# Four remainder loads on GpSimd's queue, tile 1 of x on the sync queue, and a new order of the first transposes

## The chip, the cores and the metric

The kernel runs on one core of a Trainium2 chip. The metric is the device time of one execution in microseconds. A core has a matrix engine (TensorE, PE in the profile, with its weight loads shown apart as PEld), VectorE (DVE), ScalarE (ACT), GpSimd (POOL) and SyncE (SP). Loads and stores are issued by SP, ACT or POOL into queues and are carried out by 16 DMA engines.

## The reference

An input x of 2048 tokens by 448 features is normalized; a linear attention with 16 heads of 28 and a two-layer network are applied to the result, and their product is added to x:

```python
def _A_ref(x, wqkv, wo):
    B, S, D = x.shape
    H = 16; Dh = D // H
    qkv = (lambda x, *d: x.transpose(*d))((x @ wqkv).reshape(B, S, 3, H, Dh), 2, 0, 3, 1, 4)
    q, k, v = qkv[0], qkv[1], qkv[2]
    phi = lambda t: jnp.where(t > 0, t + 1, jnp.exp(t)) + 1e-6
    pq, pk = phi(q), phi(k)
    kv = jnp.einsum("bhsd,bhse->bhde", pk, v)
    z = jnp.einsum("bhsd->bhd", pk)
    num = jnp.einsum("bhqd,bhde->bhqe", pq, kv)
    den = jnp.einsum("bhqd,bhd->bhq", pq, z)[..., None] + 1e-6
    o = num / den
    return (lambda x, *d: x.transpose(*d))(o, 0, 2, 1, 3).reshape(B, S, D) @ wo

def _B_ref(x, w1, b1, w2, b2):
    h = jnp.einsum("bsd,df->bsf", x, w1) + b1
    r = jnp.where(h > 0, h, 0)
    return jnp.einsum("bsf,fd->bsd", r * r, w2) + b2

xn = _layernorm(x)
return x + _A_ref(xn, ...) * silu(_B_ref(xn, ...))
```

The hidden width F is 1792. All inputs and the output are bf16.

## The kernel before

The 2048 tokens are 16 tiles of 128 (`NT`), four of which make a group (`NG`). Each of the first stages needs xT, the normalized x with the features on the partitions. The 448 features are three full chunks of 128 and a last one of 64. A product over 448 features therefore has three full steps and one of 64 rows. The last chunk is kept twice in xT, in rows 0 to 63 and in rows 64 to 127, and so are the last 64 rows of the weights. Two products with 64 rows each can then run side by side in the two halves of the matrix. The two copies of the last 64 weight rows are loaded apart from the main load: the code calls these two loads `twins` (L414 in `load_k`, L434 in `load_w1`).

The program is a list of operations with what they read and write. `schedule` (L88) simulates them and fixes the order of each engine's instructions: PE and SP keep the order in which the operations were added, while DVE, ACT and POOL take the operation with the earliest due time among those that are ready in the simulation. `after` and `prio` of an operation tie it to a place in that order, and they are no waits on the chip. In `schedule` a load occupies a single simulated DMA pipe (L218 to L222). `emit` (L231) turns the dependences into semaphore waits.

The change lies in the head of the program, in which the tiles 0 to 3 are handled one by one:

- Loads. `load_x(0, 1)` on SP, `load_x(1, 2, "act")` on ACT, then on SP the main k weights (`wk`, 384 KB), tiles 2 and 3, the two main loads of the first four h blocks (`w1a`, 192 KB each), the two k twins (64 KB each), the two h twins (32 KB each), tiles 4 to 7, and the remaining weights (L441 to L450).
- Statistics. `ln_stats` (L461) and `ln_rstd` (L467) give mean and 1/std of a tile: `st` and `mv` on DVE, `ln` and `ex` on ACT.
- Normalization. `ln_norm` (L482) writes features 0 to 383 of tiles 0 to 3, in two parts (256 and 128 columns) for tiles 0 and 1. `ln_last` (L506) writes the last 64 features twice, in one DVE operation of 128 columns. For tiles from 4 on, `ln_norm` writes 448 columns and `ln_twin` (L497) copies the last 64.
- Transposes. `pe_transpose` (L519) transposes the chunks of a tile on PE into a PSUM bank and copies them to xT on the engine named; `turn(si, part, eng)` (L1072) does it for half a tile. Its four operations of a tile use the names `xT00`, `xT01` and so on in the table `head`.
- First products. k of tiles 0 and 1 (`k0`, `k1`), and the first four h blocks, whose left half of 256 tokens (tiles 0 and 1) is `first` and whose right half (tiles 2 and 3) is `second`. `mains` (L596) issues full steps, `rests` (L607) the 64-row steps of two products side by side: these are the remainders, and they are the first users of the twins. After them comes `pe_four(*second)`, which needs xT of tiles 2 and 3.
- `warm` (L1056) issues matmuls on constants ahead of the first transposes.
- The two strings at L1109 and L1110 fix the order of the head's operations on DVE and ACT by name (`xd` is the doubled last chunk, `xn` the normalized part).

The masks that POOL builds (`zmask`, L383 to L387) are used in the middle of the program, at 75.9 us.

Of the kernel before, what the change touches and what calls it, by code (L numbers as in the profile page):

```python
# [10 lines left out]
S, D, F = 2048, 448, 1792  # L11
# [6 lines left out]
RATE = 300e3  # L18
# [37 lines left out]
class Program:  # L56
# [31 lines left out]
    def schedule(self):  # L88
# [59 lines left out]
        while n:  # L148
# [68 lines left out]
            op.start = st  # L217
            if op.nbytes:  # L218
                free[e] = st + op.dur
                s2 = max(dma_free, st + 1.75)  # L220
                dma_free = s2 + op.nbytes / RATE
                op.end = dma_free + 0.3  # L222
            else:
                op.end = st + du
                free[e] = op.end
# [62 lines left out]
def bass_recurrent_scan__linear_attn_block__dense_activation_squared_relu__prompt_kernel(  # L288
# [4 lines left out]
    with ExitStack() as es:  # L293
# [106 lines left out]
        def dma(eng, dst, src, writes, nbytes, reads=()):  # L400
            return add(eng, lambda e, _: e.dma_start(dst, src), reads, writes, 0.5, nbytes=nbytes)

        def load_x(lo, hi, eng="sp", reads=()):
            names = [("x", i) for i in range(lo, hi)]
            return dma(eng, x_tok[:, lo:hi, :], x_r[:, lo:hi, :], names, (hi - lo) * P * D * 2, reads)

        def load_k(eng, w, src, name, lo, hi, eng2=None, reads=(), later=False):

            n = (hi - lo) * 2
            dma(  # L410
                eng, w[:, 0:3, lo:hi], src[0:384, lo:hi].rearrange("(c p) j -> p c j", p=P), [(name, 0)], 384 * n,
                reads,
            )
            def twins():  # L414
                for i in (0, 1):
                    dma(eng2 or eng, w[64 * i : 64 * i + 64, 3, lo:hi], src[384:448, lo:hi], [(name, 1 + i)], 64 * n)

            if later:
                return twins
            twins()  # L420

        def load_w1(name, lo, hi, parts=1, between=()):


            for i in range(parts):
                n = (hi - lo) // parts
                c = slice(lo + i * n, lo + (i + 1) * n)
                dma(
                    "sp", w_1[:, 0:3, c], B_w1[0:384, c].rearrange("(c p) j -> p c j", p=P), [(name, 3 * i)], 768 * n
                )  # L430
            for todo in between:
                todo()
            mid = (lo + hi) // 2
            for i, c in ((0, slice(lo, mid)), (1, slice(mid, hi))):  # L434
                dma("sp", w_1[64 * i : 64 * i + 64, 3, c], B_w1[384:448, c], [(name, 1 + i)], 64 * (hi - lo))

        w1_of = lambda fi: "w1a" if fi < 4 else "w1b" if fi < 8 else "w1c"
        wnames = lambda name: [(name, i) for i in range(4 if name == "w1a" else 3)]
        table = add("act", lambda e, _: e.preload_act_table_set("natural_log_exp_and_others"), [], ["actw"], 0.1)
        table.prio = -120  # L440
        load_x(0, 1)  # L441
        load_x(1, 2, "act").prio = -118
        twins = load_k("sp", w_qkv, A_wqkv, "wk", 384, 2 * D, later=True)
        load_x(2, 4)
        dma("act", b1r[0:NF, :], B_b1.rearrange("(f p) -> f p", p=P), ["b1r"], F * 2, ["b1r"]).prio = -115
        load_w1("w1a", 0, 512, 2, [twins])
        load_x(4, 8)
        load_w1("w1b", 512, 1024)
        load_k("sp", w_qkv, A_wqkv, "wq", 0, 384)
# [30 lines left out]
            )  # L480

        def ln_norm(si, part=None):  # L482
            c = (slice(0, D if si > 3 else 384), slice(0, 256), slice(256, 384))[0 if part is None else part + 1]
            return add(
                "dve",
                lambda e, _: e.tensor_scalar(
                    out=xn[:, si, c], in0=x_tok[:, si, c], scalar1=mv[:, si, 0:1],
                    scalar2=rstd[:, si : si + 1], op0=ALU.subtract, op1=ALU.mult,
                ),
                [("x", si), ("mv", si), ("rstd", si)], [("xn", si) if part is None else ("xn", si, part)],  # L490
                0.4 if part is None else (0.22, 0.18)[part],
            )
# [554 lines left out]
        for i in range(4):  # L1047
            head[f"st{i}"], head[f"mv{i}"] = ln_stats(i)
            head[f"ln{i}"], head[f"ex{i}"] = ln_rstd(i, i + 1)
            for j in (0, 1) if i < 2 else (None,):  # L1050
                head[f"xn{i}" + ("" if j is None else str(j))] = ln_norm(i, j)
            twin = head[f"xd{i}"] = ln_last(i)
        for op in masks:
            op.after = [twin]

        def warm(n, wide=False, after=()):  # L1056
            b = Buf("W")
            w = 512 if wide else P

            def f(e, _):  # L1060
                for _i in range(n):
                    last = e.matmul(ps(b)[:, 0:w], junk[:, 0:P], junk[:, 0:w], start=True, stop=True)
                return last

            add("pe", f, ["ones", *after], [b], n * (0.426 if wide else 0.107))

        warm(8, wide=True)
        k0, k1 = kk(0), kk(1)
        first = [hh(0, fi, 0) for fi in range(4)]
        second = [hh(0, fi, 1, first[fi].bank) for fi in range(4)]  # L1070
# [7 lines left out]

        turn(0, 0, "act")
        turn(0, 1, "act")  # L1080
        turn(1, 0, "act")
        mains(k0, (0,), [("xT", 0, "a")] + wnames("wk")[:1])
        mains(k0, (1,), [("xT", 0, 0)])
        mains(k0, (2,), [("xT", 0, 1)])
        turn(1, 1, "act")
# [8 lines left out]
        )  # L1094
        h_mains(0, (2,))
        h_mains(1)
        h_mains(2)
        head["xT2"] = pe_transpose(2, None, "act")
        h_mains(3)
        head["xT3"] = pe_transpose(3, None, "dve")  # L1100
        n = len(pr.ops)
        rests(k0, k1)
        k0.out()
# [2 lines left out]
        rests(first[0], first[2])  # L1106
        rests(first[1], first[3])
        for eng, names in (
            ("dve", "st0 mv0 st1 mv1 xn00 xn01 xd0 xn10 xn11 xd1 st2 mv2 st3 mv3 xd2 xn2 xd3 xn3 xT3"),  # L1109
            ("act", "ln0 ex0 ln1 ex1 xT00a xT00 xT01 xT10 xT11 ln2 ex2 ln3 ex3 b1 xT2"),  # L1110
        ):
            ops = [head[n] for n in names.split()]
            for i, op in enumerate(ops):
                op.after = ops[:i]
                op.prio = -100 + i
        for op in early:
            op.after = [head["xT3" if op.eng == "dve" else "xT2"]]
        pe_four(*second)

        def quads(g, what):  # L1120
# [16 lines left out]
        for g, (first, second) in enumerate(streams):  # L1137
            if g + 1 < NG:
                n = len(pr.ops)
                ln(4 * g + 4, 4 * g + 8)  # L1140
                if g == 0:
                    for op in pr.ops[n:]:
                        if op.writes[0][0] == "st":
                            op.after = [head["xT3"]]
            quads(g, first)
            for i in range(4 * g, 4 * g + 4):
                if i:
                    zsum(i)
            if g + 1 < NG:
                for si in range(4 * g + 4, 4 * g + 8):  # L1150
                    dma_transpose(si)
                    if si == 5:
                        load_x(8, 12)
            if g == 0:
                load_x(12, 16)
                late_loads()
            quads(g, second)
            rest_transpose(2 * g)
            rest_transpose(2 * g + 1)
# [86 lines left out]
```

## Time and profile before

| What | Value |
|---|---|
| Median of 3 runs | 141.42 us (141.3 to 141.51) |
| The profiled execution, its time | 141.34 us |
| Its span on the page | 139.7 us |
| TensorE clock granted | 1.00 in every stretch |
| Data moved by DMA | 12.91 MB, mean 92 GB/s |
| DMA engines' share in the first 10 us | 0.85, 256 GB/s |
| First 10 us: busy PE, DVE, ACT, POOL | 9.51, 7.15, 6.29, 2.35 us |

The page of the profile gives busy times of the engines; a line of a group names the line of the code, the engine, the operation, the tile it writes and the tiles it reads. POOL's work in the head ends at 3.25 us, after which it has none until 66.67 us. SP's queue issues without a pause from 0.0 to about 10.8 us and then waits for work until 13.59 us. In that time it issues the four twin loads from 2.44 to 4.92 us and tiles 4 to 7 at 4.96 us.

### The profile page before, as it was taken

The numbers are of one execution on the slowest core, as the hardware profiler recorded it, in microseconds if no ns is written. First come the engines' busy times: TensorE is split into PE (matmuls) and PEld (weight loads), VectorE is DVE, ScalarE is ACT, GpSimd is POOL, SyncE is SP. The second block draws the span as 40 slices with busy tenths as digits, with TensorE's granted clock in tenths as the row PEclk, the third lists the DMA queues.
The fourth block names the chain that finished last, engine by engine and source line by source line (L and its number), as shares of the span: only waits on it lengthen the run. The fifth ranks groups of instructions, "written<-read, shape, count | busy, mean of one in ns | idle before, by whom it ended". The sixth has DMA issues, their size and how long they took to land.

```text
span 139.7 us, 3106 instructions
## 1 busy us (share of the span) xinstructions
PE 136.6 (98%) x1255; PEld 68.0 (49%) x1255; DVE 92.2 (66%) x226; ACT 77.8 (56%) x152; POOL 25.0 (18%) x33
## 2 busy tenths in 40 slices
PE   9999999999999999999999999999999999999992
PEld 2474444444444444444455455645555555555481
DVE  3989899799878994889995900329636071542653
ACT  4769787879988878979788912422033030301220
POOL 6000000000000000000893000000002328091770
DMA  6997367999723200000000148960000103111122
GB/s 190 247 335 219 77 170 186 356 276 144 131 52 70 60 6 0 0 19 5 0 0 0 42 120 169 175 107 0 0 0 5 66 0 101 35 66 66 38 99 68
DMA packets 20354, 12.91 MB, mean 92 GB/s; under 512 B 9524, under 2 KB 19956, under 8 KB 20340
## 3 DMA queue, kind: packets, MB, share of 16 engines
q1 hardware_dynamic: 18332, 11.52, 33.3%
q10 hardware_dynamic: 2008, 1.20, 4.3%
q8 instruction: 10, 0.16, 0.5%
q14 instruction: 4, 0.03, 0.1%
HBM read 8.78 MB, written 2.10 MB: 78 GB/s over the span
## 4 chain that ended last, share of the span: by engine, by line
PE 95%; DVE 2%; DMA 2%; issue 0%; DVEq 0%
PE pb L955 31%; PE pb L688 30%; PE pb L641 9%; PE pb L1021 8%; PE pb L722 7%; PE pb L672 6%; DMA x_tok<-in_A_x_dram 2%; PE pb L528 1%; PE pb L728 1%; DVE st L463 1%; PE pb L815 1%; PE pb L776 1%; PE pb L853 0%; DVE xn L991 0%; DVE mv L464 0%; PE pb L846 0%
## 5 line engine op out<-in xcount | busy, mean ns | idle before, releaser
L688 PE MATMUL pb<-xT,w 64*128 64x512 bf16 (+2 forms) x408 | 51.6, 365 | 0.0
L955 PE MATMUL pb<-w,r 64*128 64x448 bf16 (+3 forms) x406 | 44.9, 343 | 0.0
L697 ACT ACTIVATE r<-pb,b1f 128x512 bf16<-128x512 f32 x56 | 35.1, 688 | 4.2 <-PE pb L688 4.2
L688 PEld LDWEIGHTS pb<-xT,w 64*128 64x128 bf16 (+1 forms) x408 | 22.8, 94 | 22.5 <-ACT r L697 0.5
L955 PEld LDWEIGHTS pb<-w,r 64*128 64x128 bf16 (+1 forms) x406 | 22.8, 95 | 19.9 <-issue 0.7
L966 DVE TENSOR_TENSOR gbuf<-pb,b2b 128x448 bf16<-128x448 f32 (+1 forms) x16 | 9.2, 608 | 30.0 <-PE pb L955 30.0
L931 ACT ACTIVATE gbuf<-gbuf 128x448 bf16<-128x448 bf16 (+1 forms) x16 | 8.7, 565 | 36.0 <-DVE gbuf L966 35.5
L1000 POOL TENSOR_TENSOR xn<-xn,x_tok 128x448 bf16<-128x448 bf16 x15 | 15.0, 1032 | 46.3 <-DVE xn L991 46.3
L641 PE MATMUL pb<-w_qkv,xT 64*128 64x512 bf16 (+1 forms) x106 | 17.8, 376 | 0.0
L672 PE MATMUL pb<-xT,w_qkv 64*128 64x512 bf16 x84 | 15.5, 376 | 0.0
L705 DVE TENSOR_TENSOR r<-r 128x512 bf16<-128x512 bf16 x42 | 14.4, 418 | 0.0
L390 POOL MEMSET kvm<- 128x2048 bf16 x1 | 1.8, 1804 | 63.4 <-DVE zb L666 63.4
L1021 PE MATMUL pb<-msb,pqT 64*128 64x448 bf16 (+3 forms) x93 | 10.9, 343 | 0.0
L629 DVE SCALAR_TENSOR_TENSOR qk<-pb,qk 128x512 bf16<-128x512 f32 x16 | 10.6, 685 | 0.2
L463 DVE BATCH_NORM_STATS2 st<-x_tok 128x6 f32<-128x448 bf16 x16 | 9.3, 610 | 2.0 <-DMA x_tok<-in_A_x_dram 2.0
L991 DVE TENSOR_TENSOR xn<-pb,gbuf 128x448 bf16<-128x448 f32 (+2 forms) x17 | 9.2, 591 | 2.0 <-ACT gbuf L931 1.5
L619 ACT ACTIVATE qk<-pb 128x512 bf16<-128x512 f32 x16 | 8.9, 593 | 3.0 <-PE pb L641 2.5
L641 PEld LDWEIGHTS pb<-w_qkv,xT 64*128 64x128 bf16 (+1 forms) x106 | 6.7, 94 | 6.0 <-ACT xT L538 0.2
L722 PE MATMUL pb<-qk,xn 128*128 128x448 bf16 x48 | 9.3, 353 | 0.0
L619 ACT ACTIVATE pqT<-pb 128x512 bf16<-128x512 f32 x12 | 6.8, 597 | 3.2 <-PE pb L688 1.6
L672 PEld LDWEIGHTS pb<-xT,w_qkv 64*128 64x128 bf16 x84 | 6.0, 94 | 5.0
L706 ACT ACTIVATE r<-r 128x512 bf16<-128x512 bf16 x14 | 8.4, 637 | 0.0
(71 smaller groups left out, 99.7 us busy)
## 6 DMA issues: line engine op xcount, KB each, us to landing
out_dram<-xn SPq DMA_DIRECT2D x15, 112.0 KB, 1.7
w<-in_B_w_dram SPq DMA_DIRECT2D x1, 1568.0 KB, 10.0
x_tok<-in_A_x_dram SPq DMA_DIRECT2D x3, 448.0 KB, 3.8
xT<-rows ACTq DMA_DIRECT2D x6, 112.0 KB
w<-in_B_w_dram SPq DMA_DIRECT2D x1, 576.0 KB, 4.6
xT<-rows SPq DMA_DIRECT2D x5, 112.0 KB
w_o<-in_A_wo_dram SPq DMA_DIRECT2D x1, 392.0 KB, 11.3
w_qkv<-in_A_wqkv_dram SPq DMA_DIRECT2D x1, 384.0 KB, 3.6
```

The source lines that it names most:

```text
L463: add("dve", lambda e, _: e.bn_stats(st6[:, si, :], x_tok[:, si, :]), [("x", si)], [("st", si)], 0.58),
L619: add("act", lambda e, _: e.activation(out=slot, in_=src(), func=AF.Exp), [buf, "actw"], [tile], 0.6)
L629: lambda e, _: e.scalar_tensor_tensor(out=slot, in0=src(), scalar=1.0 + 1e-6, in1=slot, op0=ALU.add, op1=ALU.max),
L641: return e.matmul(ps(b)[:, 0:512], xT[half[h], c, si * P : (si + 1) * P], w_qkv[half[h], c, 384 : 2 * D], start=start, stop=stop,)
L672: return e.matmul(ps(b)[:, 0:512], w_qkv[half[h], c, m * P : (m + 1) * P], xT[half[h], c, g * 512 : (g + 1) * 512], start=start, stop=stop,)
L688: return e.matmul(ps(b)[:, c0 : c0 + n], w_1[half[h], c, fi * P : (fi + 1) * P], xT[half[h], c, t : t + n], start=start, stop=stop,)
L697: lambda e, _: e.activation(out=slot, in_=ps(b)[:, 0:512], func=AF.Relu, bias=b1f[:, fi : fi + 1]),
L705: return e.tensor_tensor(out=slot, in0=slot, in1=slot, op=ALU.mult)
L722: last = e.matmul(ps(b)[:, 0:D], xn[:, si, c * P : (c + 1) * P], pk_of(si), start=(si == 0), stop=(si == NT - 1),)
L955: return e.matmul(ps(b)[:, 0:n], r2[half[h], fi, si * P : (si + 1) * P], w_2[half[h], fi, c], start=start, stop=stop)
L1000: eng, lambda e, _: e.tensor_tensor(out=ob, in0=ob, in1=x_tok[:, si, c], op=ALU.add),
L1021: return e.matmul(ps(b)[:, 0:n], q, m, start=start, stop=stop)
```

## The change

- The k twins and the twins of `w1a` are issued on POOL instead of SP. Each now reads `("wk", 0)`, so that POOL waits until the main k weights have landed.
- The planner's model gives a load on POOL a landing 3.0 us after its start, without the shared pipe.
- Tile 1 of x is loaded on SP, directly behind tile 0, instead of on ACT.
- For tiles 1 to 3, the main normalization now writes all features (tile 1: 256 and 192 columns; tiles 2 and 3: 448) and `ln_twin` copies the last 64; tile 0 is as before. The order in the string for DVE is changed to match: `xn` ahead of `xd`.
- Two small matmuls follow the eight of `warm`.
- On PE, the first transposes of tile 1 follow the first k step of tile 0 instead of preceding it; the transposes of tile 2 precede the third h block instead of following it.
- The transposes of tile 3 are made in two halves: the first is copied by DVE, the second by ACT. What had been tied to `xT3` is tied to `xT30` on DVE, and to `xT31` on ACT where it had been tied to `xT2`.

```diff
--- before.py
+++ after.py
@@ -217,9 +217,12 @@
             op.start = st
             if op.nbytes:
                 free[e] = st + op.dur
-                s2 = max(dma_free, st + 1.75)
-                dma_free = s2 + op.nbytes / RATE
-                op.end = dma_free + 0.3
+                if e == "pool":
+                    op.end = st + 3.0
+                else:
+                    s2 = max(dma_free, st + 1.75)
+                    dma_free = s2 + op.nbytes / RATE
+                    op.end = dma_free + 0.3
             else:
                 op.end = st + du
                 free[e] = op.end
@@ -413,7 +416,7 @@
             )
             def twins():
                 for i in (0, 1):
-                    dma(eng2 or eng, w[64 * i : 64 * i + 64, 3, lo:hi], src[384:448, lo:hi], [(name, 1 + i)], 64 * n)
+                    dma(eng2 or eng, w[64 * i : 64 * i + 64, 3, lo:hi], src[384:448, lo:hi], [(name, 1 + i)], 64 * n, twin_after)
 
             if later:
                 return twins
@@ -432,18 +435,24 @@
                 todo()
             mid = (lo + hi) // 2
             for i, c in ((0, slice(lo, mid)), (1, slice(mid, hi))):
-                dma("sp", w_1[64 * i : 64 * i + 64, 3, c], B_w1[384:448, c], [(name, 1 + i)], 64 * (hi - lo))
+                dma(
+                    "pool" if name == "w1a" else "sp", w_1[64 * i : 64 * i + 64, 3, c], B_w1[384:448, c], [(name, 1 + i)],
+                    64 * (hi - lo), twin_after if name == "w1a" else (),
+                )
 
         w1_of = lambda fi: "w1a" if fi < 4 else "w1b" if fi < 8 else "w1c"
         wnames = lambda name: [(name, i) for i in range(4 if name == "w1a" else 3)]
         table = add("act", lambda e, _: e.preload_act_table_set("natural_log_exp_and_others"), [], ["actw"], 0.1)
         table.prio = -120
+        twin_after = [("wk", 0)]
         load_x(0, 1)
-        load_x(1, 2, "act").prio = -118
-        twins = load_k("sp", w_qkv, A_wqkv, "wk", 384, 2 * D, later=True)
+        load_x(1, 2)
+        twins = load_k("sp", w_qkv, A_wqkv, "wk", 384, 2 * D, "pool", later=True)
+        twin_after = [("wk", 0)]
         load_x(2, 4)
         dma("act", b1r[0:NF, :], B_b1.rearrange("(f p) -> f p", p=P), ["b1r"], F * 2, ["b1r"]).prio = -115
         load_w1("w1a", 0, 512, 2, [twins])
+        twin_after = ()
         load_x(4, 8)
         load_w1("w1b", 512, 1024)
         load_k("sp", w_qkv, A_wqkv, "wq", 0, 384)
@@ -480,7 +489,7 @@
             )
 
         def ln_norm(si, part=None):
-            c = (slice(0, D if si > 3 else 384), slice(0, 256), slice(256, 384))[0 if part is None else part + 1]
+            c = (slice(0, D), slice(0, 256), slice(256, D if si else 384))[0 if part is None else part + 1]
             return add(
                 "dve",
                 lambda e, _: e.tensor_scalar(
@@ -1049,7 +1058,7 @@
             head[f"ln{i}"], head[f"ex{i}"] = ln_rstd(i, i + 1)
             for j in (0, 1) if i < 2 else (None,):
                 head[f"xn{i}" + ("" if j is None else str(j))] = ln_norm(i, j)
-            twin = head[f"xd{i}"] = ln_last(i)
+            twin = head[f"xd{i}"] = ln_twin(i, i + 1, "dve") if i else ln_last(i)
         for op in masks:
             op.after = [twin]
 
@@ -1065,6 +1074,7 @@
             add("pe", f, ["ones", *after], [b], n * (0.426 if wide else 0.107))
 
         warm(8, wide=True)
+        warm(2)
         k0, k1 = kk(0), kk(1)
         first = [hh(0, fi, 0) for fi in range(4)]
         second = [hh(0, fi, 1, first[fi].bank) for fi in range(4)]
@@ -1078,8 +1088,8 @@
 
         turn(0, 0, "act")
         turn(0, 1, "act")
+        mains(k0, (0,), [("xT", 0, "a")] + wnames("wk")[:1])
         turn(1, 0, "act")
-        mains(k0, (0,), [("xT", 0, "a")] + wnames("wk")[:1])
         mains(k0, (1,), [("xT", 0, 0)])
         mains(k0, (2,), [("xT", 0, 1)])
         turn(1, 1, "act")
@@ -1094,10 +1104,11 @@
         )
         h_mains(0, (2,))
         h_mains(1)
+        head["xT2"] = pe_transpose(2, None, "act")
         h_mains(2)
-        head["xT2"] = pe_transpose(2, None, "act")
         h_mains(3)
-        head["xT3"] = pe_transpose(3, None, "dve")
+        turn(3, 0, "dve")
+        turn(3, 1, "act")
         n = len(pr.ops)
         rests(k0, k1)
         k0.out()
@@ -1106,15 +1117,15 @@
         rests(first[0], first[2])
         rests(first[1], first[3])
         for eng, names in (
-            ("dve", "st0 mv0 st1 mv1 xn00 xn01 xd0 xn10 xn11 xd1 st2 mv2 st3 mv3 xd2 xn2 xd3 xn3 xT3"),
-            ("act", "ln0 ex0 ln1 ex1 xT00a xT00 xT01 xT10 xT11 ln2 ex2 ln3 ex3 b1 xT2"),
+            ("dve", "st0 mv0 st1 mv1 xn00 xn01 xd0 xn10 xn11 xd1 st2 mv2 st3 mv3 xn2 xd2 xn3 xd3 xT30"),
+            ("act", "ln0 ex0 ln1 ex1 xT00a xT00 xT01 xT10 xT11 ln2 ex2 ln3 ex3 b1 xT2 xT31"),
         ):
             ops = [head[n] for n in names.split()]
             for i, op in enumerate(ops):
                 op.after = ops[:i]
                 op.prio = -100 + i
         for op in early:
-            op.after = [head["xT3" if op.eng == "dve" else "xT2"]]
+            op.after = [head["xT30" if op.eng == "dve" else "xT31"]]
         pe_four(*second)
 
         def quads(g, what):
@@ -1141,7 +1152,7 @@
                 if g == 0:
                     for op in pr.ops[n:]:
                         if op.writes[0][0] == "st":
-                            op.after = [head["xT3"]]
+                            op.after = [head["xT30"]]
             quads(g, first)
             for i in range(4 * g, 4 * g + 4):
                 if i:
```

## The prediction

> **What bounds the kernel now.** I read the page first, then the chain that ended last for the first 12 us, then each engine's order of instructions in that stretch, then the loads' landings, since the diff touches only the head and loads that the head waits for. The page gives the bound:
>
> ```profile
> PE 136.6 (98%) x1255; PEld 68.0 (49%) x1255; DVE 92.2 (66%) x226; ACT 77.8 (56%) x152; POOL 25.0 (18%) x33
> ...
> PE 95%; DVE 2%; DMA 2%; issue 0%; DVEq 0%
> ```
>
> TensorE is never without work once it has started: from 9 us to 130 us its records are gapless. A gain can therefore come only from starting this stream earlier or closing holes in the head, and a hole made in the head goes to the end undiminished. The chain shows the head; columns are start, duration and piece:
>
> ```profile
> 0.00 2.20 DMA x_tok<-in_A_x_dram
> 2.20 0.02 issue
> 2.22 0.64 DVE st L463
> ...
> 3.07 0.52 DVE st L463
> 3.59 0.02 issue
> 3.61 0.18 DVE mv L464
> 3.80 0.24 DVE xn L486
> 4.04 0.05 issue
> 4.09 1.00 PE pb L528 x6
> 5.08 0.65 PE pb L641 x3
> ...
> 8.10 0.22 PE pb L528 x4
> 8.32 0.32 PE pb L641 x2
> 8.64 1.90 PE pb L688 x32
> 10.54 0.86 PE pb L641 x8
> ```
>
> Tile 0's arrival at 2.20 starts everything. The statistics of tile 1 sit between those of tile 0 and the first normalization, so the DVE sets the 4.09. The two pieces at 8.32 and 8.64 hold the first k remainders (L641 x2), and the h remainders ahead of the second h quarter: these need the twin loads that the change moves. One hole is named by the weight loads:
>
> ```profile
> 8.84 1.42 PEld L688 LDWEIGHTS pb<-xT,w 64*128 64x128 bf16 x28 [0.26 <-DVE xT L537]
> ```
>
> The second h quarter waits for tile 3's copy (DVE, 8.36 to 8.78) and begins at 8.84. Then the twins' present landing (issue columns: count, KB each, us from issue to landing; windows at their issue):
>
> ```profile
> w_qkv<-in_A_wqkv_dram SPq DMA_DIRECT2D x2, 64.0 KB, 3.9
> ...
> w<-in_B_w_dram SPq DMA_DIRECT2D x2, 32.0 KB, 3.0
> ```
>
> Narrower windows give 2.44 + 4.1 = 6.5 us and 3.05 + 3.7 = 6.75 us for k, and 6.9 and 7.0 us for h. Their users come at 8.26 and 8.48. They are more than 1.2 us early: moving them off SP frees no wait on the path.
>
> **What the skill says.** The Trainium skill, "DMA: Bandwidth & Descriptors", section "Anatomy of one DMA — SWDGE (gpsimd) path", prices a load from GpSimd, whose descriptors software writes, at about 2.0 us plus bytes over 436 GB/s. No load here is issued there, so no trace confirms it. "Issuing engines are not separate DMA queues" on that page says that all issuers use the same 16 engines and another issuer saves issue time only; the trace agrees that issue time is the small part (0.57 us per SP issue against 2.7 to 4.1 us to land). "SBUF — State Buffer", section "SBUF: two separate sides", says that GpSimd and two-port VectorE operations exclude each other, and (in "A bandwidth-pool intuition that's wrong (but worth ruling out)") that a GpSimd load of 620 ns took 3100 ns beside one. This trace shows such exclusion for GpSimd's own operations:
>
> ```profile
> L367 POOL TENSOR_SCALAR_AFFINE_SELECT hmask<-hmask x2: 295/2377/4459, 68.7 to 73.2; 128x112 f32<-128x112 f32 x2
> ```
>
> One select took 295 ns and its equal 4459 ns, while 19 squares (L705) ran back to back on the DVE, each still 419 ns. GpSimd lost, the DVE lost nothing.
>
> **Part by part.** The sum is made against the profiled execution, 141.34 us (span 139.7 and 1.6 around it), which lies 0.08 under the median of 141.42.
>
> *x 1 on SP behind x 0.* At present the two share the engines: from 1.5 to 1.8 us SP's queue moved 0.05 MB and ACT's 0.04. Adding up the traffic in steps of 0.1 us gives 117 KB by 1.7 us, tile 0's size; shared, it needed until about 1.9. So x 0 lands some 0.2 us sooner (bounds 0 and 0.3). Tile 1, issued 0.3 later, comes at about 2.6, before the DVE wants it (2.98 less 0.2). The other side: the k main load is issued at 0.9, not 0.44. The engines stay loaded from 1.6 on, so I put it at 4.1 instead of 4.04; its user started at 4.92, or 4.7 shifted. Nothing lost. x 2 and 3 may slip from 4.71 to 4.9, just where the DVE asks; the following rstd is held by ACT until later.
>
> *Normalization.* Tiles 1 to 3 lose the doubled last chunk (312 ns) for a wider main one (374 to 392 ns for 448 columns) and a 64-column copy (181 ns by L666): about 0.11 us less DVE each. Worth nearly nothing: xn of tile 2 is started by rstd (ACT, 6.68), not by DVE time.
>
> *T 1 behind the first k main, T 2 before h 2.* Nothing is added; 0.22 us of matmul pass T 1, whose copy then ends about 0.2 later and holds k 1 by 0.1 us (cost 0.1, bounds 0 and 0.15). T 2 issued before h 2 meets xn of tile 2 just as it is ready: a hole of at most 0.1, closed because T 3 then no longer has to wait. The two small warm matmuls fill PE's idle time before 4.09 and cost at most 0.05.
>
> *T 3 in halves.* The DVE copies 256 columns instead of 512 (425 ns before; half saves about 0.15), ACT the rest in 381 ns. ACT starts later by a transpose, and T 3's second half may wait 0.05 for the bank that T 2's copy frees. The later half decides: ready at about 8.63 shifted, instead of 8.78. Together with the earlier start the head gains 0.2 us: the second h quarter could begin at 8.64. Bounds of this gain: 0.05 and 0.35.
>
> *Four twin loads on GpSimd.* They wait for the k main load, so the first can be taken up at 4.15. Behind the waiting instruction on POOL stand only the other three and the zmask operations, wanted first at 75.9. SP, relieved of four issues (2.4 us), issues x 4 to 7 and all that follows 2 us sooner; their users come late, and PE behind 9 us has no hole that this could fill. All that counts is when the last h twin, t4, is in. PE then needs 0.05 plus two paired 256-column steps (0.21) before the second quarter, which began at 8.84: the change in time is t4 - 8.58, and never better than -0.2.
> - Low: spacing as SP's, 0.57, and the skill's price of 2.15 for 64 KB (2.08 for 32): t4 = 4.15 + 1.7 + 2.1 = 8.0, in time.
> - Middle: spacing 0.8, between that 0.62 and the 1 us to the first byte that the DMA page states under Specifications, and a landing of 2.7, the shortest that the same 32 KB had on SP under this load: 4.15 + 2.4 + 2.7 = 9.25, so +0.67.
> - High: the DVE's normalizations run unbroken from 4.2 to 5.0 and from 6.6 to 7.6 in the new order; if they shut GpSimd out as L705 did, 1.2 us more: t4 = 10.5, so +1.9.
> I take the middle, since 8.0 needs the best of both and the engines move some 345 GB/s in this stretch (4.0 to 5.0 us), with 1.66 MB issued on SP by 2.9 us in the new order still ahead of or beside the twins. Result: 141.34 + 0.67 = 142.0.
>
> **The rivals.**
> 1. Twins late by a moderate amount (forecast): +0.3 to +1.1, 142.0 us. For it: four serial issues from 4.15, each needing over 2 us. Chance 0.38.
> 2. GpSimd is shut out by the DVE, or holds DVE back in turn on the first tiles: +1.2 to +2.5, about 143. For it: the 4459 ns select. Against it: statistics lie between the normalizations (5.0 to 6.4) and leave gaps for three issues. Chance 0.18.
> 3. Other side: the twins are in before PE reaches the h remainders. One mechanism, a free ring of their own instead of a place behind 384 KB of h weights, so landings of 2.1 us; it decides if t4 is under 8.4. Then the gain of x 0's earlier landing remains, -0.2 (to -0.35): 141.1. Against it: the spacing. Chance 0.24.
> 4. Gain and delay cancel (t4 near 8.6), 141.4, within the bound. Chance 0.20.
>
> **How the numbers follow.** A measurement of this kernel tells about 0.2% from no change, 0.28 us. Slower: 1 and 2 and a remnant of 4, 0.57. Rival 3 has most of its mass beyond 0.2%, counting extra gain from the earlier loads that I did not find: faster 0.20. Within: 0.23. The range takes rival 3 to -0.3 (141.05) and two thirds of rival 2 (143.1). The likeliest case alone spans 141.6 to 142.5.
>
> **What would show it.** Right: PE has a hole of 0.4 us or more between T 3 and the h remainders, put down to a w load from POOL, and the second h quarter starts after 9.1; first normalization 0.2 earlier; POOL's issues 0.6 to 1.0 apart. Wrong: remainders directly behind T 3 (then the issues or landings are cheaper than assumed), an x 0 that still lands at 2.2, DVE normalizations above 400 ns (GpSimd holding the port), or a changed time outside the span.

## The result and the profile after

The changed kernel takes 147.2 us (median of 6 runs, 145.12 to 147.82), the kernel before 141.47 us (6 runs beside it). The ratio is 1.0347, with a 95% interval of 1.0274 to 1.0421. The ratio is formed from the runs within 1.5% of the fastest of their kernel, three of the six after, so it is lower than that of the two medians. The change is slower, as forecast, but by 5.7 us where 0.67 were forecast and 1.9 was the highest case worked out. The profiled execution took 147.07 us with a span of 145.7 us. One run had a full clock and took 145.12 us, the other five had a mean clock of 0.987 or 0.988.

From the page of the kernel after (busy times, the granted clock in 40 slices, GpSimd's DMA queue, the shares of the chain of waits, and two groups whose last column is idle time and what ended it):

```profile
PE 138.4 (95%) x1257; PEld 69.2 (47%) x1257; DVE 92.7 (64%) x226; ACT 78.6 (54%) x153; POOL 27.3 (19%) x37
...
PEclk9998699999999999999999999999999999999999
...
q0 software_dynamic: 128, 0.20, 0.5%
...
PE 89%; DMA 7%; POOL 1%; SPq 1%; DVE 0%; issue 0%; DVEq 0%
...
L697 PE MATMUL pb<-xT,w 64*128 64x512 bf16 (+2 forms) x408 | 52.4, 371 | 0.6 <-DMA w<-in_B_w_dram 0.6
...
L650 PE MATMUL pb<-w_qkv,xT 64*128 64x512 bf16 (+1 forms) x106 | 18.9, 395 | 3.1 <-DMA w_qkv<-in_A_wqkv_dram 3.1
```

DMA has 7% of the chain instead of 2%, PE waits 3.7 us for weights, and the fifth clock slice shows a 6. All of that is in the head. The chain that ended last, between 0.9 and 17 us (start, duration, piece):

```profile
0.91 3.55 DMA w_qkv<-in_A_wqkv_dram
4.45 0.30 issue
4.75 1.18 POOL w_qkv L404 x2
5.93 0.50 POOL w L404
6.43 6.11 DMA w<-in_B_w_dram
12.54 0.05 issue
12.58 2.81 PE pb L697 x32
15.39 1.65 PE pb L650 x8
17.04 0.86 PE pb L697 x8
```

GpSimd takes up the first twin at 4.75, when the k weights are in, and is done with issuing in time. The fourth load then needs 6.11 us from its issue until its data is in (its landing). The piece of 32, which is four h remainders and the second h quarter behind them, starts at 12.58 instead of 8.64; here and below "the second h quarter" stands for this piece. Its 32 matmuls need 2.81 us instead of 1.90, and the eight after them 1.65 instead of 0.86. The stretches of the same trace show why (columns: stretch, busy time and count of PE, PEld, DVE, ACT, POOL, granted clock, DMA share, GB/s):

```profile
8.00:11.50 3.50, 0.53 (x6) 0.25 (x4) 1.46 (x4) 0.58 (x2) 0.85 (x4) 1.00 1.10 288
...
13.50:16.50 3.00, 3.00 (x28) 1.71 (x24) 1.63 (x5) 1.68 (x5) 0.00 (x0) 0.50 0.03 8
16.50:17.00 0.50, 0.50 (x6) 0.22 (x4) 0.49 (x2) 0.50 (x2) 0.00 (x0) 0.64 0.00 0
17.00:20.00 3.00, 3.00 (x32) 1.36 (x28) 1.76 (x6) 2.04 (x5) 0.00 (x0) 1.00 0.22 44
```

PE stands almost idle from 8.5 to 12.58, while the DMA engines are full (the share of 1.10). About a microsecond after it resumes, its clock is halved for three microseconds. So the loss has two parts, and fixed points of both traces give their sizes:

| Point | Before | After | Difference |
|---|---|---|---|
| second h quarter starts | 8.64 | 12.58 | +3.94 |
| the piece of 70 h matmuls starts | 61.27 | 66.90 | +5.63 |
| the piece of 84 h matmuls starts | 94.14 | 99.77 | +5.63 |
| span | 139.7 | 145.7 | +6.0 |

Between the first two points the loss grows by 1.69 us. The clock alone gives 3.0 x 0.50 + 0.5 x 0.36 + 0.5 x 0.05 (0.95 from 13.0 to 13.5) = 1.7 us. The last 0.4 us arise at the very end: the last store on ACT's queue (48 KB) landed 2.2 us after its issue, before 1.8. It differs from execution to execution (1.5 to 2.4 us in the runs below).

Three questions follow: why the loads of 64 and 32 KB need some 6 us on GpSimd's queue, what the halved clock costs, and what the rest of the change is worth without the four loads.

### The profile page after: what moved, and what is told of

Its sections match the earlier page's. It is cut to its first block, busy times and chain, and to the rows that moved or that the text cites. A ratio compares the mean times of both kernels' runs of the same rounds, so it can differ in the third digit from the quotient of the medians.

```text
span 145.7 us, 3108 instructions
## 1 busy us (share of the span) xinstructions
PE 138.4 (95%) x1257; PEld 69.2 (47%) x1257; DVE 92.7 (64%) x226; ACT 78.6 (54%) x153; POOL 27.3 (19%) x37
## 3 DMA queue, kind: packets, MB, share of 16 engines
q10 hardware_dynamic: 1864, 1.09, 3.7%
## 4 chain that ended last, share of the span: by engine, by line
PE 89%; DMA 7%; POOL 1%; SPq 1%; DVE 0%; issue 0%; DVEq 0%
PE pb L964 29%; PE pb L697 29%; PE pb L650 8%; PE pb L1030 7%; PE pb L731 6%; PE pb L681 6%; DMA w<-in_B_w_dram 4%; DMA w_qkv<-in_A_wqkv_dram 2%; PE pb L737 1%; POOL w_qkv L404 1%; PE pb L824 1%; PE pb L785 1%; SPq L404 1%; PE pb L862 0%; POOL w L404 0%
## 5 line engine op out<-in xcount | busy, mean ns | idle before, releaser
L697 PE MATMUL pb<-xT,w 64*128 64x512 bf16 (+2 forms) x408 | 52.4, 371 | 0.6 <-DMA w<-in_B_w_dram 0.6
L697 PEld LDWEIGHTS pb<-xT,w 64*128 64x128 bf16 (+1 forms) x408 | 23.3, 96 | 23.6 <-DMA w<-in_B_w_dram 0.9
L650 PE MATMUL pb<-w_qkv,xT 64*128 64x512 bf16 (+1 forms) x106 | 18.9, 395 | 3.1 <-DMA w_qkv<-in_A_wqkv_dram 3.1
L681 PE MATMUL pb<-xT,w_qkv 64*128 64x512 bf16 x84 | 15.5, 376 | 0.0
L631 DVE TENSOR_SCALAR qk<-qk 128x512 bf16<-128x512 bf16 x16 | 4.7, 291 | 8.0 <-ACT qk L628 8.0
```

The source lines that it names most:

```text
L650: return e.matmul(ps(b)[:, 0:512], xT[half[h], c, si * P : (si + 1) * P], w_qkv[half[h], c, 384 : 2 * D], start=start, stop=stop,)
L681: return e.matmul(ps(b)[:, 0:512], w_qkv[half[h], c, m * P : (m + 1) * P], xT[half[h], c, g * 512 : (g + 1) * 512], start=start, stop=stop,)
L697: return e.matmul(ps(b)[:, c0 : c0 + n], w_1[half[h], c, fi * P : (fi + 1) * P], xT[half[h], c, t : t + n], start=start, stop=stop,)
```

## Which part of the change costs the time

**The change without its GpSimd loads** (`sp_twins`): the four twins go back to SP, all else is kept.

```diff
-                    "pool" if name == "w1a" else "sp", w_1[64 * i : 64 * i + 64, 3, c], B_w1[384:448, c], [(name, 1 + i)],
+                    "sp", w_1[64 * i : 64 * i + 64, 3, c], B_w1[384:448, c], [(name, 1 + i)],
...
-        twins = load_k("sp", w_qkv, A_wqkv, "wk", 384, 2 * D, "pool", later=True)
-        twin_after = [("wk", 0)]
+        twins = load_k("sp", w_qkv, A_wqkv, "wk", 384, 2 * D, later=True)
+        twin_after = ()
```

> The whole change, but with the four twin loads back on SP, without a wait, in their old place behind the first h weights. Theory A (all of the loss is the twins' late landing on GpSimd's queue, with what follows from it): 141.0 to 141.5 us, second h quarter beginning at 8.6 to 8.8. Rival B (the x load on SP, the wider normalization, the moved transposes or the other order of DVE and ACT lose time of their own): above 141.8 us.

Measured: 141.59 us, ratio 1.0024 (1.0005 to 1.0043). The profiled run (141.91 us) starts the second h quarter at 9.58, not at 8.6 to 8.8 as theory A had it.

**The GpSimd loads alone** (`pool_alone`): the kernel before, with the four twins on GpSimd behind the k weights and the planner's 3.0 us for them, as in the change, and nothing else of it.

> The kernel before with one part of the change alone: the twins on GpSimd's queue behind the wait for the main k weights (and the planner's 3.0 us for them). Theory A: the whole loss is here, 146.5 to 147.8 us, k twins in at about 11.5 and h twins at about 12.5. Rival B: below 145.5 us, the rest coming from the other parts.

Measured: 145.68 us, ratio 1.0276 (1.0239 to 1.0313). The profiled run took 144.31 us at a clock of 1.00, and the second h quarter started at 12.07 (+3.43). The three other runs had a clock of 0.988 and took 145.54 to 145.89. So the four loads alone cost 4.2 of the 5.7 us, less than theory A had put here. The rest of the change alone gains nothing; if it does anything, it costs 0.1 (by the medians) to 0.3 us (by the ratio). Some 1.2 us thus arise only where both are together. Of these, 0.5 can be seen in the traces: the last twin is in at 12.54 in the kernel after and at 12.02 in `pool_alone`. Where the others come from is not shown.

## Why the twins come late

**SP stopped while the twins are under way** (`hold_sp`): in the kernel after, tiles 4 to 7 and all that SP issues behind them wait for the second of the two h twins.

```diff
-        load_x(4, 8)
+        load_x(4, 8, reads=[("w1a", 2)])
```

> The changed kernel with SP's loads from x 4 to 7 on held back until the last h twin has landed, so that only 1.2 MB are queued when GpSimd issues. Theory D (the twins' first packets come only when the bytes that SP queued earlier are through, and then share the engines with the rest): first k twin lands within 3 us of its issue, all four by 8.5 us, before PE asks for them. Rival E (a fixed price of GpSimd's path, whatever else is queued): landings still 5.5 us or more after issue, the last at about 12.5. The time is not the aim: the second h group's weights come late, 142.5 to 145 under D, 149 or more under E.

Measured: 142.93 us (two runs, 142.31 and 143.54). The issues of GpSimd in that trace (queue, count, KB each, us from issue to landing):

```profile
w_qkv<-in_A_wqkv_dram POOLq DMA_DIRECT2D x2, 64.0 KB, 2.1
w<-in_B_w_dram POOLq DMA_DIRECT2D x2, 32.0 KB, 2.4
```

The same loads in the kernel after:

```profile
w_qkv<-in_A_wqkv_dram POOLq DMA_DIRECT2D x2, 64.0 KB, 6.2
...
w<-in_B_w_dram POOLq DMA_DIRECT2D x2, 32.0 KB, 6.0
```

GpSimd issues that second h twin first in this run, at 4.61, so SP goes on at 6.77. But its loads move only 0.03 MB from 7 to 8 us, and by then both k twins are in. With the engines nearly free, a twin on GpSimd needs 2.1 to 2.6 us. So neither GpSimd nor its path is slow by itself; what makes the difference is SP's traffic. That can act in two ways: by what SP had issued before the twins, or by what it issues after them. The next runs try to separate the two.

**SP stopped after its second h weights** (`stop_after`): as before the twins, SP issues tiles 4 to 7 and the main load of `w1b` early, and then nothing until the second h twin is in (10.1 us).

```diff
-                    64 * (hi - lo), twin_after if name == "w1a" else (),
+                    64 * (hi - lo), twin_after if name == "w1a" else [("w1a", 2)] if name == "w1b" else (),
```

> The changed kernel in which SP issues up to the main load of the second h group (some 0.95 MB still to move when GpSimd issues at 4.75), and the rest only when the last h twin has landed. Theory D (what SP queued before GpSimd's issue goes first): first packets of GpSimd's queue at 7.5 to 8.0 as in the change, twins landing 4 us or more after issue. Theory I (what counts is that SP goes on issuing and moving beside it): first packets before 6.5, landings within 3 us. The held loads cost time of their own, some 142 to 145 us in all.

**SP goes on once GpSimd has issued** (`behind_pool`): tiles 4 to 7 wait for a small memset on GpSimd that stands behind its four loads. What SP issues then is younger than all of the twins.

```diff
...
+        mark = pool(lambda e, _: e.memset(mark_t[:, :], 1.0), ["mark"], [("wk", 0)], dur=0.1)
+        mark.prio, mark.after = 1.0, issued
-        load_x(4, 8)
+        load_x(4, 8, reads=["mark"])
```

> The counterpart: SP holds x 4 to 7 and the rest until GpSimd has issued all four twins (about 6.8 us), so that hardly anything is ahead of them and everything comes behind. Theory D: first packets near 5.7, k twins within 2.5 us of issue; h twins, issued last, at most 3.5 us. Theory I: the h twins, which meet SP's new stream, take 5 us again while the k twins, already moving, take 2.5.

One run each, 144.97 us and 143.06 us. The twins' rows in `stop_after`:

```profile
w_qkv<-in_A_wqkv_dram POOLq DMA_DIRECT2D x2, 64.0 KB, 4.5
w<-in_B_w_dram POOLq DMA_DIRECT2D x2, 32.0 KB, 4.6
```

and in `behind_pool`:

```profile
w_qkv<-in_A_wqkv_dram POOLq DMA_DIRECT2D x2, 64.0 KB, 2.2
w<-in_B_w_dram POOLq DMA_DIRECT2D x2, 32.0 KB, 2.0
```

The first packets of GpSimd's queue, and what SP's queue moved beside them, by stretches (MB):

| Stretch | after: SP / GpSimd | stop_after: SP / GpSimd | behind_pool: SP / GpSimd |
|---|---|---|---|
| 5 to 6 us | 0.29 / 0 | 0.33 / 0 | 0.22 / 0 |
| 6 to 7 us | 0.37 / 0 | 0.36 / 0 | 0.00 / 0.08 |
| 7 to 7.5 us | 0.16 / 0 | 0.18 / 0 | 0 / 0.05 |
| 7.5 to 8 us | 0.18 / 0 | 0.16 / 0.04 | 0 / 0.03 |
| 8 to 8.5 us | 0.12 / 0.05 | 0.03 / 0.11 | 0.01 / 0.03 |
| 8.5 to 9 us | 0.11 / 0.04 | 0.01 / 0.03 | 0.06 / 0 |
| 9 to 10 us | 0.19 / 0.08 | 0.00 / 0.01 | 0.30 / 0 |

In the kernel after, the twin issued at 4.75 moves no byte before 8.0. By 4.75 SP had issued 2.1 MB (two small loads of 0.03 MB each are left out of the sum), of which 0.96 MB had moved; 1.14 MB was ahead. From 4.75 to 8.0 the engines moved 1.09 MB. In `stop_after` the same backlog is through at the same time, and with nothing issued later the twins then go nearly alone. In `behind_pool` only some 0.2 MB is ahead. SP's younger loads there move their first 0.01 MB between 8.0 and 8.5, when the twins are all but in, so this run does not tell what younger loads do to a twin under way. By these single runs the landing of 6 us consists of 2.0 to 2.2 us of its own, some 2.4 us more behind older loads (4.5 in `stop_after`), and some 1.5 us more of sharing with loads that SP issued after 4.75. For the later twins, a part of those was older too.

SP's own queue was no better off. Two 32 KB loads for `w1b`, which SP issued in the kernel after between 3.9 and 4.6 us, just ahead of GpSimd's first, took as long as the twins:

```profile
w<-in_B_w_dram SPq DMA_DIRECT2D x2, 32.0 KB, 6.3
```

**Another queue instead of GpSimd's** (`k_on_act`): the k twins are issued by ACT at 4.80, the h twins by GpSimd at 4.64.

```diff
...
-        twins = load_k("sp", w_qkv, A_wqkv, "wk", 384, 2 * D, "pool", later=True)
+        twins = load_k("sp", w_qkv, A_wqkv, "wk", 384, 2 * D, "act", later=True)
...
+        for op in on_act:
+            op.after, op.prio = [head["xT01"]], -150
```

> The changed kernel with the two k twins issued by ACT behind its first three copies of xT (about 5.2 us, with the wait for the k weights), the h twins on GpSimd as in the change. Both sets then meet the same queue of SP. Theory G (the delay belongs to GpSimd's queue, whose loads start late while SP's flow): the k twins land 2.5 to 4.0 us after their issue, as SP's own did before, the h twins 5 to 6 us after theirs. Theory H (any second queue that is filled behind SP's backlog waits that long): both take 5 us or more.

Measured: 146.93 us (one run). Issue to landing in its trace:

```profile
w_qkv<-in_A_wqkv_dram ACTq DMA_DIRECT2D x2, 64.0 KB, 6.3
...
w<-in_B_w_dram POOLq DMA_DIRECT2D x2, 32.0 KB, 6.0
```

Both queues wait alike, and both see their first packets between 7.5 and 8 us. Which engine issued made no difference in this run.

**SP's later loads tied to the k weights too** (`gate_wk`): tiles 4 to 7 wait for the same load as the twins, so both sides start together.

```diff
-        load_x(4, 8)
+        load_x(4, 8, reads=[("wk", 0)])
```

> The changed kernel with SP's loads from x 4 to 7 on waiting for the main k weights too, as GpSimd does, so that when the twins are issued (4.6 to 6.7) some 0.2 MB of older loads and then 448 KB of x 4 to 7 are ahead of them instead of 0.95 MB. Theory D in numbers: first packets of GpSimd's queue at 6.2 to 7.0 instead of 8.0, k twins in at 7.8 to 9.3, h twins at 8.5 to 10; 142 to 144 us. Rival E: first packets at 8.0 again, k twins after 11.

Measured: 145.58 us (two runs, clock 0.988). The twins land 4.9 to 5.0 us after issue, the last at 11.49, and their first packets come at about 7.8. All of that is later than theory D's numbers: 0.71 MB was still ahead at GpSimd's first issue (4.86), and in a lull of SP's traffic from 5.5 to 6.5 the engines moved only 0.19 MB; by 7.5 they had moved 0.75 MB. So the first packet again came when the older backlog was through. Why the engines moved so little in the lull, and GpSimd's loads nothing, is open.

**The place in line alone** (`sp_late`): the kernel before, with its twins on SP, but behind the 0.85 MB of tiles 4 to 7 and `w1b` that they used to precede. No other queue, no wait.

```diff
...
-        load_w1("w1a", 0, 512, 2, [twins])
...
+        load_w1("w1a", 0, 512, 2)
         load_x(4, 8)
-        load_w1("w1b", 512, 1024)
+        load_w1("w1b", 512, 1024, 1, [twins, h_twins])
```

> The kernel before with one edit: its four twin loads stay on SP, but are issued behind the main load of the second four h blocks, so behind the 0.85 MB (tiles 4 to 7, w1b) that they passed. No other queue and no wait for the k weights. Theory D (loads go in order of issue, the place in line is what counts): issued at 4.5 to 6.3, landing 3.0 to 4.5 after issue, the last in at 9 to 10.5, so the second h quarter some 0.7 to 2.2 us later and 142.0 to 143.8 at full clock. Rival M (within one queue the place costs little, a second queue is what is slow): last twin in by 8.5, under 141.8.

Measured: 142.62 us, ratio 1.0088 (1.0075 to 1.0101), clock 1.00. Its chain, the last issue and what follows:

```profile
5.32 4.89 DMA w<-in_B_w_dram
10.21 0.05 issue
10.25 1.92 PE pb L694 x32
```

The last twin now needs 4.89 us on SP as well, and the second h quarter starts 1.61 us late. So a place further back is dear on SP's own queue too. It costs 1.2 us here; in the change the wait for the k weights puts the twins further back still (issue from 4.75 on instead of 3.45), and SP, relieved of four issues, is further ahead.

**No wait** (`no_wait`): the kernel after, with the twins issued at once, from 0.86 us on.

```diff
-        twin_after = [("wk", 0)]
+        twin_after = ()
...
-        twin_after = [("wk", 0)]
+        twin_after = ()
```

> The changed kernel without GpSimd's wait for the main k weights: the four twins are issued from about 0.5 us on. Theory D (a load on GpSimd's queue moves after the bytes that SP had queued when it was issued, of which there are then hardly any): twins in by 5.5 us, no wait at the remainders; 141.3 to 142.2 us, the k weights and x somewhat later for the shared engines. Rival E2 (the queue of GpSimd yields to SP's whole backlog, also to what is issued after it): twins land after 9 us and the time stays above 144.

Measured: 142.41 us, ratio 1.0059 (1.0037 to 1.0081). The twins are in by about 7.6, two microseconds later than theory D had it, and PE waits for none of them. The head's stall is then at the k weights, which land at 5.04:

```profile
0.92 4.12 DMA w_qkv<-in_A_wqkv_dram
5.04 0.14 issue
5.18 0.58 PE pb L650
```

The second h quarter starts at 9.61, in `sp_twins` at 9.58, and PE's work is alike in both to the end. In these two traces GpSimd's queue without the wait costs nothing in the head, and gains nothing. The medians still differ by 0.8 us (142.41 and 141.59). The profiled run is 0.66 us longer than that of `sp_twins`, and its last store took 2.4 us instead of 1.7; that the store accounts for the medians too is not shown.

This run also limits the account given so far. The twins needed 4.4 and 5.1 us here, and their first packet came at 3.3, 2.4 us after the first issue at 0.86. Only 0.23 MB (tiles 0 and 1) had been issued before that, but SP had moved 0.4 MB by 3.3. So a part of the k weights, whose issue began 0.06 us after GpSimd's, went ahead of the twins as well, and loads issued later seem to slow them too.

## What the halved clock costs

**Filler matmuls in the hole** (`filled`): 14 wide matmuls on constants ahead of the remainders keep PE busy while it waits.

```diff
         n = len(pr.ops)
+        warm(7, wide=True)
+        warm(7, wide=True)
         rests(k0, k1)
```

> The changed kernel with 14 matmuls on constants (some 3.0 us) between the transposes of tile 3 and the remainders, so that TensorE isn't idle while it waits for the twins. Theory C (1.7 to 2.0 of the 6 us are the halved TensorE clock between 13.3 and 16.9 us, brought on by the idle wait): 145.0 to 145.5 us, granted clock 1.00 throughout, the twins landing as late as before. Rival (the clock dip has nothing to do with the wait): 147 us and the dip still there.

Measured: 146.7 us, ratio 1.0359 (1.0337 to 1.0381), clock 1.00 in three runs of four; the fourth had 0.988 and took 149.8 us, and no trace of it was kept. In the profiled run the dip is gone, the loss is not: the planner counts the fillers and orders DVE and ACT differently, and PE then waits 1.4 us for ACT at 21.45.

**The same without a price in the planner** (`filled2`): 18 filler matmuls of 384 columns with a modelled duration of 0.

```diff
...
+        def busy(e, _):
+            for _i in range(18):
+                last = e.matmul(ps(t30)[:, 128:512], junk[:, 0:P], junk[:, 0:384], start=True, stop=True)
+            return last
...
+        add("pe", busy, [("xT", 3, 0)], [], 0.0)
```

> The changed kernel with 18 matmuls of 384 columns on constants (2.9 us) in the wait for the k twins, written to a bank that is free, at no cost to the planner, so that the other engines keep their order (in the first such run they did not). Theory C (some 1.8 of the 6 us are the halved TensorE clock after the idle wait): 145.0 to 145.6 us, granted clock 1.00 from 13 to 17 us, twins as late as before. Rival: 146.7 or more, so that the clock dip would be no cost of its own.

Measured: 146.73 us, ratio 1.0363 (1.0339 to 1.0386), clock 1.00 in the profiled run. From the second h quarter to the piece of 70 it takes 53.30 us, against 54.32 in the kernel after and 52.64 in `pool_alone` at full clock. So with PE kept busy the clock stayed up in three runs of four (the fourth: 0.987, 149.3 us), but the expected time was missed: in the profiled execution the last twin landed at 13.13, and a changed order on ACT cost 0.6 to 0.7 us at 42 us.

The size of the clock's part therefore rests on other traces, not on the fillers. From the second h quarter to the piece of 70 the eight traces at full clock in which SP's later loads were not held back and no fillers were added (`before`, `pool_alone`, `sp_late`, `sp_twins`, `no_wait`, `x_act`, `old_order`, `whole_t3`) take 52.57 to 52.65 us. The three in which the clock fell to half take 54.32 (`after`), 54.32 (`gate_wk`) and 54.14 (`k_on_act`). A dip thus costs 1.5 to 1.7 us. The times agree: the run of the kernel after at full clock took 145.12 against 147.07 to 147.82 of the others, and `pool_alone` 144.31 against 145.54 to 145.89. That idleness brings the dip on is supported by where it occurs, in the kernels with long waits, but the two low runs with fillers leave it short of shown.

## What the rest of the change is worth

**Tile 1 of x back on ACT** (`x_act`), on top of `sp_twins`:

```diff
-        load_x(1, 2)
+        load_x(1, 2, "act").prio = -118
```

> The changed kernel with the four twins back on SP and tile 1 of x back on ACT, so that only the normalization, the moved transposes, the halved copy of tile 3 and the two small warm matmuls remain of the change. In the run with the twins on SP and x 1 on SP too, PE waited 0.4 us for the k weights and DVE 0.6 us for tiles 2 and 3. Theory F (x 1 on SP, 0.46 us of issue ahead of the k weights, costs what that run lost): 141.1 to 141.45 us, first k product at 4.7 to 4.9, second h quarter at 8.6 to 8.7. Rival (the moved transposes or the order of DVE and ACT cost it): 141.6 or more again.

**The old places of the transposes of tiles 1 and 2 on PE too** (`old_order`), on top of `x_act`:

```diff
+        turn(1, 0, "act")
         mains(k0, (0,), [("xT", 0, "a")] + wnames("wk")[:1])
-        turn(1, 0, "act")
...
-        head["xT2"] = pe_transpose(2, None, "act")
         h_mains(2)
+        head["xT2"] = pe_transpose(2, None, "act")
```

> As the run with twins on SP and x 1 on ACT (0.23% slower than before), but with PE's old places for the transposes of tile 1 and tile 2; the normalization, the halved copy of tile 3 and the small warm matmuls stay. Theory J (the moved transposes make k 1, T 2 and T 3 wait, 0.1 us each, as their traces' chains show against that of before): 141.2 to 141.5 us, no difference from before. Rival K (the halved copy or the normalization itself costs it): 141.65 or more.

**Tile 3 whole again** (`whole_t3`), on top of `old_order`; only the normalization and the two small warm matmuls then differ from the kernel before:

```diff
-        turn(3, 0, "dve")
-        turn(3, 1, "act")
+        head["xT3"] = pe_transpose(3, None, "dve")
...
```

> old_order with the transposes of tile 3 made whole and copied by DVE, as in the kernel before. Against that kernel only the normalization of tiles 1 to 3 and the two small warm matmuls differ now. Theory K (the halved copy, whose second half waits for the bank of tile 2, is what costs the remaining 0.3 us): 141.3 to 141.55, second h quarter within 0.15 us of the 8.64 of the kernel before. Rival L (the later 64-column copies of the normalization delay the transposes): 141.65 or more, and the wait ahead of the transposes of tile 1 or 2 is put down to the copies.

| Kernel | Time | Ratio to before | First transposes | Second h quarter |
|---|---|---|---|---|
| before | 141.34 (profiled) | | 4.09 | 8.64 |
| sp_twins | 141.59 | 1.0024 (1.0005 to 1.0043) | 3.98 | 9.58 |
| x_act | 141.72 | 1.0023 (1.0008 to 1.0038) | 4.29 | 9.05 |
| old_order | 141.77 | 1.0020 (1.0001 to 1.0038) | 4.32 | 9.28 |
| whole_t3 | 141.43 | 1.0001 (0.9990 to 1.0012) | 4.28 | 9.07 |

The places are those of the one profiled run each; tile 0 landed at 2.40 to 2.43 us in the last three, at 2.20 in the kernel before. Neither tile 1's queue nor the old order with it brings the 0.3 us back, against what theories F and J expected. With tile 3 whole they are gone. In `old_order` the halves of tile 3 show what they wait for (chain of waits):

```profile
8.02 0.60 ACT xT L547
8.63 0.05 issue
8.67 0.29 PE pb L537 x2
8.96 0.32 PE pb L650 x2
```

The second half needs a bank that ACT's copy of tile 2 still holds until 8.63. But the intervals of `old_order` and `whole_t3` overlap, and the profiled run of `whole_t3` reaches its second quarter at 9.07, not within 0.15 us of 8.64 as expected; the head differs by such amounts from run to run. That the halved copy costs the 0.3 us is what the times suggest, and is not shown.

## Why the prediction was wrong

- **The reading of the bound held.** PE had no slack in the head, a hole there goes to the end, and the remainders are the place where the change decides. The hole came where it was foretold. The larger part of it (3.06 us) was a wait for a k twin, which the prediction had not set apart, and 0.60 us for the last h twin.
- **The formula held for the wait.** The change was to be t4 - 8.58, where t4 is the time at which the last h twin is in. It landed at 12.54, which gives 3.96; the second h quarter moved by 3.94.
- **The step that failed is the landing of 2.7 us in the middle case of "Four twin loads on GpSimd".** t4 was put at 4.15 + 2.4 + 2.7 = 9.25; it was 4.75 + 1.68 + 6.11 = 12.54. The first take-up was 0.6 later (k weights in at 4.46, 0.30 us to the issue), the spacing 0.56 instead of 0.8, and the landing 3.4 us longer. The first two differences nearly cancel. The 2.7 was a landing on SP for loads in their old place, with less ahead of them. The prediction did name 1.66 MB "ahead of or beside the twins", but only to prefer the middle to the low case. It also took the wrong amount: 1.66 MB is all that SP was to issue by 2.9, moved or not. What counts is what is issued and not yet moved when GpSimd issues, 1.14 MB at 4.75. Divided by the 345 GB/s that stand beside it in the prediction, that is 3.3 us, so the first packet at 8.05; it came at 8.0. The high case, 10.5, charged DVE for the delay and not this backlog.
- **A term was missing: the clock.** An idle PE was priced at its idle time alone. The halved clock added 1.69 us in the profiled run.
- **GpSimd shut out by DVE (rival 2) did not occur.** Its four issues took 0.50 to 0.67 us each, as on SP, in the middle of the normalizations. The other direction did show, but small: the two normalizations of 448 columns in the head took 458 and 454 ns, above the 400 named as a sign, against 394 in `sp_twins`. That is 0.06 us each, and PE waited for loads, not for them.
- **A free ring of their own (rival 3) is refuted as long as older loads are under way.** Landings of 2.0 to 2.6 us appear only where SP is stopped (`hold_sp`, `behind_pool`).
- **The head's gain of 0.2 did not show.** Tile 0 landed 0.07 us sooner (statistics at 2.15 instead of 2.22) and the first transposes started at 4.00. But "nothing lost" was wrong for the k weights. From 2 to 3 us the engines moved 0.13 MB instead of 0.27, and the k weights landed at 4.46, not at 4.1; in `sp_twins`, at about 5.0. The ten traces with tile 1 on SP all have 0.11 to 0.17 MB in that stretch, the six with it on ACT 0.24 to 0.32. Why is open.
- **The halves of tile 3** were to be 0.15 us faster. The bank that was charged at 0.05 held the second half longer.

The two statements of the Trainium skill about the loads fared differently. "DMA: Bandwidth & Descriptors", in "Anatomy of one DMA — SWDGE (gpsimd) path", prices 64 KB at an estimated 2.15 us, and the runs with SP stopped agree (2.1 and 2.2 us). In "Queues, rings and completion order" the same page says that each engine goes round-robin between the queues it has work for, packet by packet. Here GpSimd's and ACT's queues moved nothing for some 3 us while SP's moved 1.1 MB, and shared only then (0.05 MB beside 0.12 from 8.0 to 8.5). The measurement decides: here a second queue was no way past older loads. On the clock, "TensorE: Matmul & The Clock Gate", Part 1, says that the clock is halved after at least one idle window of about 3.4 us, and that this window runs freely and does not restart with the kernel. This case agrees only in part. The clock fell to 0.50 after waits of 3.06 and 0.60 us, but also after a single wait of 2.71 (`k_on_act`) and after 1.48 and 0.68 us (`gate_wk`). After 2.70 and 0.43 us (`pool_alone`) it fell in three runs of four by the mean clock, after 1.74 us (`stop_after`, one run) and 1.38 us (`sp_late`) in none. No wait here was 3.4 us long, so waits well under that length were enough.

## What to carry to other kernels

Before moving a load to another queue, count what is issued before it on all queues and not yet moved, and divide by the rate of that stretch. That estimates its earliest first packet, on whichever queue it is: 8.05 against a measured 8.0 in the kernel after. It can come later; in `no_wait` it did by more than a microsecond. In these runs a wait in front of a load's issue gave its place in line to everything that SP issued in the meantime. And a hole in PE of some microseconds may be paid twice, the second time in clock.

## What the runs showed of the hardware

- A load on a second queue, GpSimd's or ACT's, got its first packet about 3 us after issue with some 1.1 MB of older loads ahead. With little ahead, GpSimd's got it about 1.4 us after issue (`behind_pool`, issued at 5.09, first packets at about 6.45).
- After holes of 3.06 and 0.60 us in PE's work the clock did not fall at once: PE ran a microsecond at 1.00 or 0.95 (from 12.58 to 13.5), then three at 0.50. In `gate_wk`, 1.48 and 0.68 us of waiting were enough: the clock was 0.65 from 12.0 to 12.5 and 0.50 from then to 15.5.
- Two loads of 112 KB one behind the other on SP, with a large load behind them, moved 133 GB/s from 2 to 3 us in the kernel after; with the second on ACT it was 274 GB/s in the kernel before. The engines' busy share was 0.89 and 0.96.
